# First K block ahead of the constants, issue time of transfers in the scheduler's costs, and the second K/V load behind a LayerNorm's rsqrt

## The chip, the cores and the metric

One core of a Trainium2 chip. The metric is the device time of one execution in microseconds. A run gives that time, the span between its first and last instruction (about 1.8 us less) and the mean clock that TensorE was granted, as a share of full speed.

## The reference, cut to what matters

The kernel computes the forward pass and all gradients of a gated block. The part that the change touches:

```python
xn = layernorm(A_q)                       # 2048 tokens x 512
k_shift = sum_t k_pad[:, t:t+S] * shift_k[:, 3-t]       # four taps along the tokens
kv = k_shift * v
y = irfft(rfft(kv, 2S) * rfft(ssm_k, 2S))[:S] + kv * ssm_D   # a long convolution for each channel
s = xn * y
h = sigmoid(xn @ w_gate) * (xn @ w_up)
out = A_q + s * silu(h @ w_down)
# and the gradients of q, k, v, shift_k, ssm_k, ssm_D, w_gate, w_up, w_down for a given grad_out
```

The Fourier transforms are matmuls against constants made on the chip. The 512 channels go in four groups of 128; the tokens in 16 blocks of 128.

## The kernel before

The kernel first records all its operations, then a list scheduler puts them into one order, with costs that its author wrote down; then it emits them. So any change of a cost or of the recorded order can deal the operations of all engines anew. The cost of a transfer, and when the scheduler believes it to have landed:

```python
def dcost(self, alt):
    ...                                   # nb bytes; run = contiguous bytes
    return (0.56 if eng == "gpsimd" else 0.4), d      # time on the issuing queue, time of the transfer

# in order():
    if op.dma:
        occ, d = self.dcost(alt)
        t = max(t, pipe - 9.0)
        pipe = max(pipe, t + 1.0) + d
        fin = pipe + 1.0
```

The start (K/V loads are issued by GpSimd; `after` is a value that a load waits for; the LayerNorm's rsqrt is a power on GpSimd):

```python
def ld_kv(cg, after=None):
    kh, vg = stA["kh", cg], stA["vg", cg] = kh_r.next(), vg_r.next()
    ...
    if after is not None:
        nc.vector.tensor_copy(kh[0:1, 3, 0:1], after)
        nc.vector.tensor_copy(vg[0:1, 0, 0:1], after)
    nc.gpsimd.dma_start(kh[:, 3:, :], kC[:, :, c0:c1])
    ...
    nc.gpsimd.dma_start(vg, vC[:, :, c0:c1])

def f_ln(i, part=None):
    ...
    nc.gpsimd.tensor_tensor(out=rstd_all[:, i:i + 1], in0=st[:, 8:9], in1=neghalf, op=ALU.pow)

ld_kv(0, wg[0:1, 2, 0:1])
ld_kv(1, wg[0:1, 2, 0:1])
...
make_identity(nc, ident)
f_ln(SEQ[0])
gen_fft_consts(nc, ar, ia, ib, negpi, Cf, BD, R)
f_ln(SEQ[1])
```

The convolution runs as streams side by side. Two of them: `acc` is one buffer: group 2's first multiply overwrites what group 1's store is still reading.

```python
def strK():
    for cg in range(NG):
        KT = stA.pop(("KT", cg))
        nc.vector.tensor_tensor(KT[:, 0:1], KT[:, 0:1], Dcol_b[:, cg:cg + 1], ALU.add)   # the D tap
        KC = KC_r.next()
        for jh in range(2):
            pt = ps_tr([8, 128], name="ps_kt")
            for jj in range(8):
                nc.tensor.transpose(pt[:, jj, :], KT[:, 8 * jh + jj:S:16], ident)
            nc.evac(KC[:, 8 * jh:8 * jh + 8, :], pt[:], 1024)
            yield 1024
        ...

def strV():
    for cg in range(NG):
        acc = acc_r.next()                                # the ring has one buffer
        for lag in (3, 2, 1, 0):
            ...
            if lag == 3:
                nc.vector.tensor_tensor(acc, src, skl, ALU.mult)
            else:
                nc.vector.tensor_tensor(term, src, skl, ALU.mult)
                nc.vector.tensor_tensor(acc, acc, term, ALU.add)
        nc.gpsimd.dma_start(ksh_d[cg], acc.rearrange("p j d -> p (j d)"))
        nc.vector.tensor_tensor(kvt, acc, vg, ALU.mult)
        ...                                               # step1, flip
```

## Time and profile before

| | before |
|---|---|
| time, 3 runs | 548.42 us (548.23 to 548.76) |
| span of the profiled run, clock | 546.9 us, 0.999 |
| TensorE idle, all | 26.6 us |
| of it 0 to 20 us | 7.7 us |
| of it 40 to 100 us | 7.4 us |
| longest pause of TensorE from 25 us to its last matmul | 0.9 us |

The lines behind these numbers stand in the prediction. From 200 to 520 us TensorE is busy 99%, and from 190 to about 385 us its order is the same in all kernels of the table below (each of its weight loads comes earlier or later by one and the same time, within 0.25 us).

Besides busy time I use one derived number below, the **lead**: the matmul work that TensorE has begun by a time T, in us, less what the kernel before has begun by then. It is counted from the weight loads, of which each trace without added matmuls has 5517, at 58 ns for a matmul of 128 columns and 216 ns for one of 512. A lead of 1.6 at 30 us means that TensorE is 1.6 us further in its work than the kernel before was at 30 us. Matmul records are not used for it: the trace before lacks 59 of them. The gaps that they leave count as idle time in the table above.

### The profile page before, as it was taken

How to read it: one execution, taken by the hardware profiler on the slowest of the kernel's cores; microseconds unless marked ns; L12 is line 12 of the kernel's file. 1: busy time of each engine (PE TensorE's matmuls, PEld its weight loads, DVE VectorE, ACT ScalarE, POOL GpSimd, SP SyncE). 2: the span in 40 equal slices, each digit the busy share in tenths (PEclk: the TensorE clock that was granted, in tenths of full speed). 3: DMA queues.
4: the chain of work that ended last, by engine and by line, in shares of the span. 5: the costliest groups of instructions: out<-in, count | busy, mean ns of one | idle time of the engine just before them, and what ended most of it. 6: DMA issues, size and time to landing. Idle time of an engine off the chain costs nothing.

```text
span 546.9 us, 13392 instructions
## 1 busy us (share of the span) xinstructions
PE 520.3 (95%) x5458; PEld 371.5 (68%) x5517; DVE 457.2 (84%) x841; ACT 347.1 (63%) x455; POOL 151.0 (28%) x260
## 2 busy tenths in 40 slices
PE   5899888999999999999999999999999999999996
PEld 3897787898688566777665666655766666665643
DVE  9699999767797998898989989829969999999550
ACT  8879899877886334544433345348777877765521
POOL 3626333304212222312222211220141051241221
PEclk9999999999999999999999999999999999999999
DMA  8999898867522998989979999999876479867422
GB/s 286 249 222 301 235 232 198 272 195 197 196 83 77 264 202 236 260 145 244 258 179 176 274 190 306 292 321 271 255 251 191 144 224 347 276 205 235 128 93 90
DMA packets 119007, 120.35 MB, mean 220 GB/s; under 512 B 76613, under 2 KB 97185, under 8 KB 118946
## 3 DMA queue, kind: packets, MB, share of 16 engines
q1 hardware_dynamic: 102514, 67.03, 50.4%
q0 software_dynamic: 15904, 52.47, 32.2%
q8 instruction: 43, 0.70, 0.5%
q14 instruction: 18, 0.15, 0.1%
q10 hardware_dynamic: 528, 0.00, 0.0%
HBM read 54.23 MB, written 47.55 MB: 186 GB/s over the span
## 4 chain that ended last, share of the span: by engine, by line
PE 66%; DVE 16%; issue 8%; ACT 5%; POOL 2%; DMA 1%; POOLq 0%; DVEq 0%; ACTq 0%
PE psum L519 66%; DVE slab L519 16%; ACT slab L519 5%; DMA ksh_d<-slab 1%; POOL out_dram L519 1%; POOL slab L519 1%; ACT L519 0%; POOLq L1451 0%; POOL KK_d L519 0%; POOLq L519 0%; DVEq L519 0%; ACTq L519 0%; POOLq L1440 0%
## 5 line engine op out<-in xcount | busy, mean ns | idle before, releaser
L519 PE MATMUL psum<-slab 128*128 128x128 bf16 (+3 forms) x5458 | 520.3, 256 | 21.7 <-ACT slab L519 11.5
L519 PEld LDWEIGHTS <-slab 128*128 128x128 bf16 (+2 forms) x5517 | 371.5, 102 | 170.1 <-issue 17.5
L519 DVE TENSOR_TENSOR slab<-slab 128x512 bf16<-128x512 bf16 (+7 forms) x467 | 300.1, 685 | 15.1 <-ACT slab L519 8.3
L519 ACT CAST slab<-psum 128x1024 bf16<-128x1024 f32 (+4 forms) x260 | 214.2, 866 | 80.2 <-PE psum L519 72.4
L519 ACT COPY slab<-psum 128x1024 bf16<-128x1024 bf16 (+2 forms) x82 | 68.5, 861 | 85.5 <-PE psum L519 85.2
L519 POOL DMA_DIRECT2D out_dram<-slab x75 | 44.9, 598 | 196.8 <-ACT slab L519 100.9
L519 DVE TENSOR_TENSOR slab<-psum,slab 128x512 bf16<-128x512 f32 (+3 forms) x84 | 63.7, 761 | 17.5 <-PE psum L519 10.0
L519 ACT ACTIVATE slab<-slab 128x512 bf16<-128x512 bf16 (+3 forms) x46 | 36.8, 805 | 18.4 <-DVE slab L519 17.8
L519 ACT ACTIVATE slab<-psum 128x512 bf16<-128x512 f32 (+1 forms) x64 | 37.3, 585 | 10.0 <-PE psum L519 8.1
L519 DVE SCALAR_TENSOR_TENSOR slab<-slab 128x1 f32<-128x1 f32 (+3 forms) x64 | 28.0, 438 | 15.7 <-ACT slab L519 12.5
L519 POOL DMA_DIRECT2D KK_d<-slab x32 | 17.3, 542 | 46.0 <-ACT slab L519 37.6
L519 DVE COPY slab<-psum 128x1024 bf16<-128x1024 bf16 (+2 forms) x34 | 21.0, 636 | 8.1 <-PE psum L519 7.8
L519 POOL DMA_DIRECT2D slab<-in_A_q_dram x29 | 16.0, 553 | 31.8 <-DMA out_dram<-slab 20.8
L519 DVE TENSOR_SCALAR slab<-slab 128x1 f32<-128x1 f32 (+7 forms) x72 | 20.5, 319 | 0.5 <-PE psum L519 0.2
L519 DVE CAST slab<-psum 128x1024 bf16<-128x1024 f32 (+1 forms) x13 | 14.8, 1141 | 4.7 <-PE psum L519 4.5
L519 DVE SCALAR_TENSOR_TENSOR slab<-psum,slab 128x512 f32<-128x512 f32 x16 | 11.0, 688 | 7.1 <-PE psum L519 6.9
L519 POOL DMA_DIRECT2D slab<-in_A_k_dram x16 | 14.9, 930 | 7.1 <-DVE slab L519 3.9
L519 POOL TENSOR_TENSOR slab<-slab 128x1 f32<-128x1 f32 x16 | 10.6, 663 | 13.6 <-DVE slab L519 13.3
L519 POOL DMA_DIRECT2D slab<-in_grad_out_dram x16 | 8.6, 539 | 17.7 <-DMA out_dram<-slab 11.6
L519 DVE BATCH_NORM_STATS2 slab<-slab 128x6 f32<-128x512 bf16 x16 | 10.9, 683 | 0.0
L519 POOL DMA_DIRECT2D slab<-sF_d x7 | 3.8, 537 | 22.7 <-DVE slab L519 18.5
L519 POOL MEMSET slab<- 1x384 bf16 (+3 forms) x16 | 5.9, 376 | 14.5 <-DVE slab L519 11.3
(21 smaller groups left out, 45.4 us busy)
## 6 DMA issues: line engine op xcount, KB each, us to landing
KK_d<-slab POOLq DMA_DIRECT2D x32, 256.0 KB, 4.0
slab<-KK_d SPq DMA_DIRECT2D x16, 512.0 KB, 6.5
out_dram<-slab POOLq DMA_DIRECT2D x58, 128.0 KB, 4.4
hS_d<-slab SPq DMA_DIRECT2D x16, 352.0 KB, 3.3
dgS_d<-slab SPq DMA_DIRECT2D x16, 352.0 KB, 3.9
duS_d<-slab SPq DMA_DIRECT2D x16, 352.0 KB, 3.7
slab<-in_A_k_dram POOLq DMA_DIRECT2D x8, 512.0 KB, 7.2
slab<-hS_d SPq DMA_DIRECT2D x8, 512.0 KB, 5.8
```

The source lines that it names most:

```text
L519: getattr(getattr(self.nc, eng), meth)(*[place(v) for v in a], **{x: place(v) for x, v in k.items()})
```

## The change

Its intent: give TensorE the first K block's transposes while the constants are still being made; tell the scheduler that a GpSimd issue with many short runs takes 1.17 us, not 0.56; and keep the second K/V load's two issues from standing in front of the first LayerNorm work that needs GpSimd.

```diff
+        soft = 0.56 if nb < 600 * run else 1.17
...
-        return (0.56 if eng == "gpsimd" else 0.4), d
+        return (soft if eng == "gpsimd" else 0.4), d
...
     ld_kv(0, wg[0:1, 2, 0:1])
-    ld_kv(1, wg[0:1, 2, 0:1])
...
     f_ln(SEQ[0])
+    nc.vector.tensor_tensor(stA["KT", 0][:, 0:1], stA["KT", 0][:, 0:1], Dcol_b[:, 0:1], ALU.add)
+    KC = stA["KC"] = KC_r.next()
+    for jh in range(2):
+        pt = ps_tr([8, 128], name="ps_kt")
+        for jj in range(8):
+            nc.tensor.transpose(pt[:, jj, :], stA["KT", 0][:, 8 * jh + jj:S:16], ident)
+        nc.evac(KC[:, 8 * jh:8 * jh + 8, :], pt[:], 1024)
...
     f_ln(SEQ[1])
+    ld_kv(1, rstd_all[0:1, SEQ[1]:SEQ[1] + 1])
...                                  # in strK: the add and the transposes only for cg > 0
```

Below, A is the K block's work ahead, B the issue time, C the second load behind the rsqrt.

More of the change, by code (lines that the diff above doesn't have):

```diff
@@ L917, in strK @@
             KT = stA.pop(("KT", cg))
-            nc.vector.tensor_tensor(KT[:, 0:1], KT[:, 0:1], Dcol_b[:, cg:cg + 1], ALU.add)
-            KC = KC_r.next()
-            for jh in range(2):
+            if cg > 0:
+                nc.vector.tensor_tensor(KT[:, 0:1], KT[:, 0:1], Dcol_b[:, cg:cg + 1], ALU.add)
+            KC = KC_r.next() if cg > 0 else stA["KC"]
+            for jh in range(2 if cg > 0 else 0):
                 pt = ps_tr([8, 128], name="ps_kt")
```

## The prediction

> **What bounds the kernel now.** I read the busy shares first.
>
> ```profile
> PE 520.3 (95%) x5458; PEld 371.5 (68%) x5517; DVE 457.2 (84%) x841; ACT 347.1 (63%) x455; POOL 151.0 (28%) x260
> ```
>
> TensorE (PE) is busy for 520.3 of 546.9 us, so 26.6 us is all its idle time: no change of order can win more unless it also makes matmuls run closer together. The next question is where the 26.6 us lie. The table of busy time by stretches gives it (columns after the stretch: its length, then busy us and instructions of PE, PEld, DVE, ACT, POOL, then granted clock, DMA share, GB/s):
>
> ```profile
> 0.00:10.00 10.00, 3.64 (x20) 2.11 (x20) 9.01 (x34) 7.65 (x8) 3.73 (x16) 1.00 0.73 255
> 10.00:20.00 10.00, 8.62 (x121) 7.93 (x119) 7.34 (x34) 8.35 (x10) 7.06 (x6) 1.00 1.04 294
> ...
> 50.00:60.00 10.00, 8.30 (x103) 6.66 (x103) 10.00 (x12) 9.22 (x11) 3.29 (x7) 1.00 0.88 298
> ```
>
> The first 20 us lack 7.7 us of PE (10 - 3.64 and 10 - 8.62). In 40 to 100 us PE lacks another 7.4 us with VectorE (DVE) at 92 to 100%: there PE waits for the two engines that empty PSUM. From 200 to 520 us PE is at 98.7 to 100% and lacks 3.3 us; the last 27 us lack 5.0. So the change, whose named parts all lie in the first 25 us, works on the largest gap.
>
> Next, the instructions of that stretch in order of time, engine by engine (start, busy us, engine, operation, count, idle before it and what ended the idle):
>
> ```profile
> 8.97 3.43 ACT L519 ACTIVATE slab<-slab 128x2048 bf16<-128x2048 int32 x3 [0.81 <-DVE slab L519]
> 12.47 1.01 ACT L519 COPY slab<-psum 128x1024 bf16<-128x1024 bf16 x1
> ...
> 19.31 0.81 ACT L519 ACTIVATE slab<-slab 128x512 bf16<-128x512 bf16 x1 [1.22 <-DVE slab L519]
> 20.14 1.28 ACT L519 ACT_TABLE_LOAD   x1
> ```
>
> ```profile
> 12.75 1.20 POOL L519 DMA_DIRECT2D slab<-in_A_k_dram  x1
> 13.94 2.28 POOL L519 DMA_DIRECT2D slab<-in_A_v_dram  x1
> 16.20 1.15 POOL L519 DMA_DIRECT2D slab<-in_A_k_dram  x1
> 17.34 1.15 POOL L519 DMA_DIRECT2D slab<-in_A_v_dram  x1
> 18.51 0.57 POOL L519 TENSOR_TENSOR slab<-slab 128x1 f32<-128x1 f32 x1
> ```
>
> ```profile
> 16.31 3.45 PE L519 MATMUL psum<-slab 128*128 128x128 bf16 x59 [0.31 <-DMA slab<-in_A_ssm_k_dram]
> 20.18 1.63 PE L519 MATMUL psum<-slab 128*128 128x128 bf16 x25 [0.42 <-ACT slab L519]
> 22.56 2.62 PE L519 MATMUL psum<-slab 128*128 128x128 bf16 x42 [0.76 <-ACT slab L519]
> ```
>
> The reader is to see one chain. The 0.57 us instruction at 18.51 is the power -1/2 (the rsqrt) of the second token block's LayerNorm. Its input was ready when DVE had added epsilon, about 15.5, but GpSimd (POOL) works in order and was issuing four K/V loads. DVE then waited 2.38 us for the rsqrt (to 19.12), ScalarE (ACT) 1.22 us for DVE; the normalised block was done at 20.12, the PE transposed it at 20.18, ACT loaded the sigmoid table, and the next PE work began at 22.56. The chain that ended last agrees: it runs through DVE to 16.15, POOL 16.20 to 19.09, DVE, ACT to 22.52, PE.
>
> **What the Trainium skill says.** "PSUM — Partial Sum Buffer", section "Engine vs sequencer instructions", has the ACT, DVE and GpSimd queues strictly first in, first out; the trace agrees, as the rsqrt stood 3 us behind two load issues it does not need. "SBUF — State Buffer", section "Who interferes with whom", has GpSimd blocked while DVE uses a two-port mode for copies and tensor_scalar; the issue at 13.94 took 2.28 us against 1.15 to 1.20 for its three likes, while DVE ran small copies and tensor_scalars, which fits. "ScalarE: Activation LUTs", section "What ACT_TABLE_LOAD costs", gives 1283 ns for a load; the trace has 1.28 us, at 20.14, and this stays.
>
> **The change part by part.**
>
> *Second load behind the rsqrt.* In the built program after, POOL has the rsqrt of block two directly after the first V load, and the second K and V issues behind it. That takes 1.15 + 1.15 = 2.3 us from in front of it: it can start when the issue of 13.94 ends, about 16.2, and end at 16.8. Its statistics also move up on DVE (ahead of the mask multiply), so the input is no bound. The second K/V data come later by about the rsqrt, 0.6 us: issues at 17 and 18.2, landing after about 10 us (10.0 and 10.4 before), so by 29; the second V group starts its arithmetic on DVE only after the first group's, whose own first multiply is at 30.59. Hidden, with over 10 us to spare.
>
> *K transposes and D-tap ahead.* The 0.15 us add moves on DVE from 10.30 to about 7.8; K block 0, issued at 1.56 and landing 4.5 to 6.5 us later, has arrived by 8.1 at the latest. Sixteen transposes follow, so PE gets K work in the gap that ended at 8.22, and ACT copies the first half between the two large sine activations, filling the 0.81 us in which it waited for DVE. But this is a move, not a removal: before the second LayerNorm ACT has, before and after, two sines of 2.0, one of 0.8, one normalisation of 0.8, five copies of 1.0 and one of 0.6. Summing from 6.16 with no gaps: 2.0 + 1.0 + 0.8 + 1.0 + 2.0 + 0.8 + 0.6 + 3.0 = 11.2, so 17.4, and with 0.6 for the first copy's wait for transposes, about 18.0. DVE also takes two first-step evictions (1.22 us each by the row of float casts) in place of cheaper copies; its queue from 11.4 on (where its float constants were done before) is then 1.2 for an eviction, 1.1 for the statistics and small copies, 1.2 for the other eviction, 0.8 for the mask multiply and 0.7 + 0.8 for the thirteen small constants, which ends near 17.2, behind the rsqrt. So ACT, not the rsqrt, becomes the last of the chain: the second normalisation starts near 18.1 instead of 19.31.
>
> Sum at the start: 19.31 - 18.1 = 1.2 us. In addition PE has about eight more 58 ns matmuls (59 in 3.45 us) behind it at the point where it transposes block two (143 against 135 in the built order), another 0.5. That is 1.2 to 1.7 us earlier into a stage that is then PE- or DVE-bound, and all of it should reach the end, because nothing after it is tied to an absolute time.
>
> *Issue time in the order.* This changes no instruction, only what the list scheduler believes an issue costs on POOL when there are 600 or more runs: 1.17 us for 0.56. The trace says the new figures are true:
>
> ```profile
> L519 POOL DMA_DIRECT2D KK_d<-slab x14 | 7.6, 543 | 10.7 <-ACT slab L519 10.6
> L519 POOL DMA_DIRECT2D slab<-in_A_k_dram x2 | 2.4, 1182 | 4.0 <-DVE slab L519 3.9
> ```
>
> It bears on the strided K, V, and paired output transfers. In the built programs PE's order of operations is identical from about 45 to 85% of its instructions; the first 45% (the convolution with the forward half) and the last 15% are dealt anew. In the first of these PE idles some 10 us in all outside the start (1.2 from 20 to 40, 7.4 from 40 to 100, 2.0 from 100 to 200); a better-timed order could win 1 to 2, a worse one lose as much. I put +0.5 us of gain on it, for truer figures and for K work running ahead, which feeds the flips and the spectral products earlier. In the tail the last 60 or so matmuls are the same and back to back, so nothing large.
>
> Together: 1.5 + 0.5 = 2.0 on 548.42, so 546.4; I lean a little further, to 546.0, because the K load of block two can also be issued some 2 us earlier (it was issued at 12.47, when block 0's transposes were done) and a wait of PE at 16.31 ended with that load.
>
> **The rivals.** First, the wait is replaced one for one: ACT or the DVE constants simply end the same chain at 19, and the gain is under 0.5 us: 548. For it speaks that ACT and DVE are both 80% busy or more in the first 20 us; against it, ACT had 1.22 + 0.81 + 0.35 us of idle time there, which are removed. Second, the first 1.5 us are won but the redealt first 45% loses them, because DVE is full from 50 us on, so that an early K stream only fills PSUM and waits: 548 to 550. For it speaks DVE at 100% in 50 to 60 us; against it, DVE is only 68% busy in 20 to 30, so its queue too can begin earlier. Third, the redealt order happens to fit much better, and half of the 7.4 us of 40 to 100 us goes: 542 to 543. For it speaks that POOL's order was made with a wrong cost; against it, POOL is only 28% busy and waits mostly for ACT and DVE. Fourth, K block 0 lands late and the early add stalls DVE and all constants behind it; the landing times above make this at most some tenths.
>
> **Range and chances.** The start is worth 0.5 to 2.5 us, the redealt order +2 to -3, which gives 542 to 549 for 8 in 10. Two per cent is 11 us: it would take over 40% of PE's idle time to be faster by that, and a new stall of a kind that I see no cause for to be slower. Faster 0.03, same 0.95, slower 0.02.
>
> **What would show it.** Right: the second normalisation on ACT starts at 17.5 to 18.7; POOL's rsqrt stands before the second K issue and no longer makes DVE wait 2 us; the PE stretch without gaps that began at 22.56 begins near 21; PE busy stays at 518 to 521 and the idle sum falls by about 2; from 200 us on all is the same but shifted. Wrong: DVE idle near 7.8 behind K block 0; the idle of 40 to 100 us above 8 or below 5; a new wait of V group two for its data near 40 us.

## The result, and the profile after

The changed kernel took 547.54 us (546.69 to 548.90, four runs) against 548.46 us (548.23 to 548.76) in the same rounds: a ratio of 0.9985, 95% interval 0.9964 to 1.0006. Ratios here are taken from the runs of the same rounds, so not quite the ratio of the medians that I quote. The interval holds 1, so these four runs alone show no difference. The gain of the medians is 0.9 us where 2.4 were forecast; the time lies in the forecast range. Two repeats (below, `again` and `again2`) put it at 1.7 and 0.1 us.

The start first. The busy time by stretches of the changed kernel (length, busy us and instructions of PE, PEld, DVE, ACT, POOL, then granted clock, DMA share, GB/s):

```profile
0.00:10.00 10.00, 4.04 (x25) 2.67 (x26) 9.02 (x35) 7.68 (x9) 4.17 (x16) 1.00 0.74 255
10.00:20.00 10.00, 8.09 (x125) 7.80 (x123) 9.07 (x35) 9.21 (x10) 5.46 (x6) 1.00 1.02 295
50.00:60.00 10.00, 7.10 (x92) 5.76 (x90) 9.97 (x12) 9.72 (x13) 4.95 (x8) 1.00 0.95 265
```

And the changed kernel's instructions in order of time, ScalarE, GpSimd and TensorE (start, busy us, engine, operation, count, idle before it and its cause):

```profile
17.36 1.02 ACT L520 COPY slab<-psum 128x1024 bf16<-128x1024 bf16 x1
18.26 0.83 ACT L520 ACTIVATE slab<-slab 128x512 bf16<-128x512 bf16 x1
```

```profile
16.20 0.74 POOL L520 TENSOR_TENSOR slab<-slab 128x1 f32<-128x1 f32 x1
18.36 1.19 POOL L520 DMA_DIRECT2D slab<-in_A_k_dram  x1 [1.41 <-DVE slab L520]
```

```profile
13.62 1.07 PE L520 MATMUL psum<-slab 128*128 128x128 bf16 x16 [0.80 <-DVE slab L520]
15.80 14.41 PE L520 MATMUL psum<-slab 128*128 128x128 bf16 x249 [1.11 <-DVE slab L520]
```

The second LayerNorm's normalisation, at 19.31 before, is at 18.26 (forecast: near 18.1); ScalarE reaches it without idle, so ScalarE's own work is now the last of the chain, as forecast. The rsqrt is at 16.20, two us before the second load's issue. From 15.80 TensorE runs without a pause past 30 us (the view ends there), where before it stopped at 20 and 22 us. The lead is 1.62 us at 30 us: in the forecast "1.2 to 1.7". So the start came out as forecast; whether for the forecast reason, the parts alone will show.

Then 50 to 60 us: TensorE is busy 7.10 us where it was 8.30. The pauses, of TensorE in the changed kernel:

```profile
55.03 0.59 PE L520 MATMUL psum<-slab 128*128 128x512 bf16 x2 [1.00 <-ACT slab L520]
57.53 2.73 PE L520 MATMUL psum<-slab 128*128 128x512 bf16 x29 [1.91 <-DVE slab L520]
...
102.51 1.68 PE L520 MATMUL psum<-slab 128*128 128x128 bf16 x23 [1.55 <-DVE slab L520]
```

The kernel before has no pause this long after 25 us. The lead over the run: 1.62 at 30 us, 2.32 at 50, 0.30 at 65, 3.82 at 100, 1.80 at 110, 1.14 at 190 and 1.58 at 500. Between 190 and 460 us each operation of TensorE comes earlier than before by the same time, 1.34 us within 0.04. So what is left at 190 does reach the end unchanged, and the start's 1.6 us is almost gone at 65. That the lead at the end is again about the start's is no proof that it is the same 1.6 us: the redealt order between gains and loses more than that.

The pause at 102.51 is another transfer: VectorE waits 1.74 us, to 101.17, for a block of x issued at 95.78. In `again` the same place cost some 0.3 us of lead, not 2.0, so it varies from run to run.

### The profile page after: what moved, and what is told of

Its sections match the earlier page's. It is cut to its first block, busy times and chain, and to the rows that moved or that the text cites. A ratio compares the mean times of both kernels' runs of the same rounds, so it can differ in the third digit from the quotient of the medians.

```text
span 545.7 us, 13451 instructions
## 1 busy us (share of the span) xinstructions
PE 522.2 (96%) x5517; PEld 371.1 (68%) x5517; DVE 459.1 (84%) x839; ACT 349.1 (64%) x457; POOL 150.5 (28%) x260
## 4 chain that ended last, share of the span: by engine, by line
PE 73%; DVE 11%; issue 8%; ACT 3%; DMA 2%; POOL 2%; POOLq 0%; DVEq 0%; ACTq 0%
PE psum L520 73%; DVE slab L520 11%; ACT slab L520 3%; POOL out_dram L520 1%; DMA ksh_d<-slab 1%; DMA slab<-in_A_q_dram 1%; POOL slab L520 0%; POOL KK_d L520 0%; POOLq L1460 0%; POOL sF_d L520 0%; POOL hF_d L520 0%; POOLq L520 0%; DVEq L520 0%; ACTq L520 0%; POOLq L1449 0%
## 5 line engine op out<-in xcount | busy, mean ns | idle before, releaser
L520 PE MATMUL psum<-slab 128*128 128x128 bf16 (+4 forms) x5517 | 522.2, 257 | 18.2 <-DVE slab L520 10.5
L520 DVE TENSOR_TENSOR slab<-slab 128x512 bf16<-128x512 bf16 (+6 forms) x467 | 300.4, 686 | 10.2 <-ACT slab L520 4.8
L520 ACT CAST slab<-psum 128x1024 bf16<-128x1024 f32 (+5 forms) x255 | 210.0, 861 | 79.4 <-PE psum L520 70.8
L520 ACT COPY slab<-psum 128x1024 bf16<-128x1024 bf16 (+2 forms) x88 | 74.9, 868 | 87.5 <-PE psum L520 87.3
L520 ACT ACTIVATE slab<-slab 128x512 bf16<-128x512 bf16 (+3 forms) x47 | 37.8, 807 | 15.3 <-DVE slab L520 14.7
L520 POOL DMA_DIRECT2D KK_d<-slab x32 | 19.3, 632 | 48.4 <-ACT slab L520 33.0
L520 DVE CAST slab<-psum 128x1024 bf16<-128x1024 f32 (+1 forms) x18 | 20.9, 1163 | 4.9 <-PE psum L520 4.0
L520 DVE COPY slab<-psum 128x1024 bf16<-128x1024 bf16 (+2 forms) x28 | 16.9, 623 | 6.5 <-PE psum L520 6.4
L520 POOL TENSOR_TENSOR slab<-slab 128x1 f32<-128x1 f32 x16 | 13.3, 844 | 15.4 <-DVE slab L520 15.2
L520 POOL DMA_DIRECT2D slab<-in_A_v_dram x6 | 7.9, 1323 | 2.5 <-DVE slab L520 1.3
```

The costliest lines, as they stand in the source:

```text
L520: getattr(getattr(self.nc, eng), meth)(*[place(v) for v in a], **{x: place(v) for x, v in k.items()})
```

## The experiments

Eighteen experiments ran, all with a correct result. Two questions were asked. What does each part do alone? And where does the lead go after 30 us?

| kernel | parts | time, us: median (range) | ratio to before, 95% | lead at 30 / 65 / 100 / 500 us |
|---|---|---|---|---|
| again | ABC | 546.90 (546.30 to 548.66) | 0.9973 [0.9953, 0.9992] | 1.45 / -0.57 / 3.26 / 2.66 |
| again2 | ABC | 548.26 (546.88 to 550.01) | 0.9983 [0.9948, 1.0018] | 1.45 / -0.86 / 2.58 / 2.01 |
| p_A | A | 551.13 (550.84 to 552.19) | 1.0043 [1.0023, 1.0064] | 0.41 / -0.71 / -1.22 / -3.02 |
| p_B | B | 547.09 (546.16 to 551.12) | 0.9982 [0.9955, 1.0009] | 1.91 / 0.15 / 3.82 / 2.44 |
| p_C | C | 549.32 (546.92 to 552.84) | 1.0011 [0.9979, 1.0042] | 1.68 / -2.55 / -1.10 / -1.30 |
| p_AB | AB | 549.14 (546.64 to 553.14) | 1.0011 [0.9978, 1.0045] | 1.59 / -0.46 / 2.46 / 0.71 |
| p_AC | AC | 548.35 (547.89 to 548.97) | 0.9991 [0.9976, 1.0006] | 0.12 / 0.19 / 1.19 / 0.05 |
| p_BC | BC | 554.22 (547.49 to 556.36) | 1.0064 [1.0024, 1.0104] | 1.33 / -4.00 / -6.14 / -7.72 |
| n1 | none; 0.58 for 0.56 | 546.55 (546.40 to 551.29) | 0.9971 [0.9943, 0.9999] | 0.00 / 0.00 / 2.78 / 2.22 |
| n5 | none; 0.26 for 0.25 | 548.62 (548.07 to 550.26) | 1.0000 [0.9981, 1.0018] | 0.06 / -0.49 / 0.66 / 0.22 |

The lead is that of the one profiled run, which need not be a median run; the profiled run of p_BC counts as slow (its time, 556.36, is over 1.5% above the fastest of that kernel), its five fast runs, 547.5 to 554.7, are what its ratio rests on.

### The change again

`again` and `again2` are the changed kernel, nothing edited.

> The changed kernel again, unaltered, for a narrower interval. From the two traces: PE is 1.6 us of matmul work ahead of the kernel before at 25 to 35 us, 3.8 ahead at 100 us, 1.8 ahead at 105 us, 1.3 to 1.5 ahead from 150 us to the end. Theory (the start is won and a stall near 101 us gives most of the rest back): 546.6 to 547.6 us, 0.9 to 1.9 us under the kernel before. Rival (the gain is run-to-run noise of the granted clock, 0.995 in three of the four runs): the interval contains no difference.

> The changed kernel unchanged, beside the three with fills. Both theories: runs with a mean clock of .999 or more at a span near 545.0, the others (.994 to .996) at 545 to 547; median 546.8 to 547.5.

Measured: 546.90 and 548.26 us. `again2`'s clocks are mixed: one run at 1.0 (span 545.1), the others at .991 to .997 (545.3 to 548.2); its median lies above the forecast 546.8 to 547.5. Of the three intervals only that of `again` lies wholly below 1. So the gain is small and unsteady.

### Each part alone, and two at a time

```diff
# p_A:  only the lines of the change in the start and in strK
# p_B:  only
+        soft = 0.56 if nb < 600 * run else 1.17
-        return (0.56 if eng == "gpsimd" else 0.4), d
+        return (soft if eng == "gpsimd" else 0.4), d
# p_C:  only
-    ld_kv(1, wg[0:1, 2, 0:1])
+    ld_kv(1, rstd_all[0:1, SEQ[1]:SEQ[1] + 1])     # moved behind f_ln(SEQ[1])
```

> Only the K transposes and the D-tap ahead. In the built order ScalarE here runs two sigmoids ahead of the second LayerNorm, which VectorE makes instead, although the rsqrt still stands behind four load issues. Theory (what wins the start is the table load and the first sigmoids ahead of the late rsqrt): PE 1.2 to 2.0 us ahead at 30 us. Rival (the rsqrt's place on GpSimd is what counts): no lead at 30 us, within 0.4. At the end: 546.5 to 548.5 in either, by how the rest is dealt.

> Only the new issue time in the order. Theory: the second LayerNorm's rsqrt still waits behind four load issues on GpSimd, so PE's lead at 30 us is 0 within 0.4 us, and any difference at the end (within 1.5 us either way) is made after 30 us by the redealt order. Rival (the truer cost lets the scheduler deal a better convolution stage): PE 1 us or more ahead at 190 us, 547.4 or less.

> Only the second K/V load behind the rsqrt. In the built order the second LayerNorm stands ahead of the table load on ScalarE, as in the kernel before, but the rsqrt comes two load issues (2.3 us) earlier. Theory (the start is held by the table load and sigmoids behind ScalarE's queue of copies, not by the rsqrt): lead of PE at 30 us 0 to 0.8. Rival (my prediction: the rsqrt was the chain's wait): lead 1.0 to 1.7 us. End: 547 to 549.

> The two source moves (K transposes with D-tap ahead; second K/V load behind the rsqrt) without the new issue time in the order. Theory (the start's gain comes from these two, the issue time only redeals the order): PE 1.2 to 1.9 us ahead at 30 us, as in the changed kernel; the time anywhere from 545.5 to 548 by how the order is dealt. Rival (the issue time is what makes the gain): no lead at 30 us, 548 or more.

> Two of three parts: K block 0's work ahead and the issue time, second K/V load where it was. Theory (the true issue time is what moves the start, in whatever company): lead of TensorE over the kernel before of 1.2 to 2.0 us at 30 us, median 547.0 to 547.8. Rival (a redealt order is worth anything from -2.5 to +1.5 us whatever was the reason to deal it anew): no particular number, 546.5 to 551; the early K work alone cost 2.5 us and could do so again (549.5 to 551).

> Issue time and the second K/V load behind the rsqrt, K block 0's work where it was. Theory: both take the same wait (VectorE's for the rsqrt) off the path, so they don't add: lead at 30 us 1.7 to 2.2, not 3.6; median 546.7 to 547.3, as the issue time alone (547.09). Rival (they add): lead 3 us or more, 545.5. Rival (redealing): 547 to 550, and a wait of VectorE at the landing of the first group's spectra store says why.

Measured: the table. Three things follow.

First, each of B and C wins the start alone (1.91 and 1.68 us at 30 us), and together they don't add (1.33, and 1.62 with A). C does it as forecast. B does it otherwise: the rsqrt is still late in p_B, but with issues that it knows to be long, the scheduler gives the second block's normalisation to VectorE, so that ScalarE, with the table load and two sigmoids, waits for no rsqrt. ScalarE and then VectorE in p_B:

```profile
17.79 1.28 ACT L520 ACT_TABLE_LOAD   x1
19.08 1.08 ACT L520 ACTIVATE slab<-psum 128x512 bf16<-128x512 f32 x2
```

```profile
19.30 0.41 DVE L520 TENSOR_SCALAR slab<-slab 128x512 bf16<-128x512 bf16 x1
```

Second, A wins little at the start (0.41, and 0.12 with C), and alone the kernel is slower by 2.5 us; why is open. K work in an early gap of TensorE is not what the start's gain came from. Nor do the two source moves A and C together make it, as was forecast: p_AC has both, and its rival came true (no lead, 548 us or more). Its second normalisation starts at 17.21, a microsecond earlier than in the changed kernel. But it still waits 1.54 us for VectorE, and an accumulator copy (the CAST at 17.93) that TensorE needs stands behind it. ScalarE and TensorE in p_AC:

```profile
17.21 0.81 ACT L519 ACTIVATE slab<-slab 128x512 bf16<-128x512 bf16 x1 [1.54 <-DVE slab L519]
```

```profile
18.97 11.26 PE L519 MATMUL psum<-slab 128*128 128x128 bf16 x190 [1.03 <-ACT slab L519]
```

So the start of the normalisation does not set the lead; what ScalarE has to hold back for it does. In the changed kernel two accumulator copies of ScalarE (at 16.45 and 17.36) stand ahead of it.

Third, the end does not follow the start. p_C changes nothing in the order of TensorE and ScalarE, and little on VectorE and GpSimd; its lead of 1.68 us is -2.55 at 65 us. p_BC loses 5.3 us between 30 and 65, behind a pause of 3.31 us that ends on ScalarE; what dealt it so is open. All of the six but p_B came out slower than their theories forecast.

### Is it the true figure, or any figure?

B's gain could come from 1.17 us being true, or from the cards being dealt anew. Two controls deal them anew with figures that have no truth in them:

```diff
# n1
-        return (0.56 if eng == "gpsimd" else 0.4), d
+        return (0.58 if eng == "gpsimd" else 0.4), d
# n5
-LATE = 0.25
+LATE = 0.26
```

> Control: the kernel before with the scheduler's cost of every GpSimd issue 0.58 us for 0.56, a change with no truth in it, that deals most of TensorE's order anew all the same. Theory (the issue time of the change gains because 1.17 is true, and puts the sigmoids ahead of the late LayerNorm): no start gain, lead at 30 us within 0.5 of 0, median 548.0 to 549.3. Rival (redealing alone moves the time by as much as the change did): median off the kernel before by 0.9 us or more, either way.

> Second control: the kernel before with the scheduler's share for late transfers 0.26 for 0.25; a different order again, no truth in it. Theory: lead at 30 us within 0.5 of 0, median 548.0 to 549.3. Rival: off the kernel before by 0.9 us or more, either way.

Measured: n1 546.55 us, as good as anything, with no start gain at all (lead 0.00 at 30 and at 65 us); n5 548.62, as before. My theory falls here: the truth of the figure is not needed for the gain. n1 wins its time between 65 and 100 us. The stretches of the kernel before, then of n1:

```profile
85.00:90.00 5.00, 4.03 (x49) 2.99 (x48) 4.97 (x7) 4.76 (x8) 2.12 (x4) 1.00 0.64 215
90.00:95.00 5.00, 4.07 (x51) 3.38 (x51) 5.00 (x9) 5.00 (x8) 2.17 (x5) 1.00 1.16 195
```

```profile
85.00:90.00 5.00, 4.68 (x62) 3.78 (x61) 4.76 (x8) 5.00 (x8) 2.73 (x5) 1.00 0.83 271
90.00:95.00 5.00, 5.00 (x73) 4.39 (x72) 4.85 (x8) 4.95 (x7) 1.49 (x3) 1.00 1.24 137
```

TensorE's busy time in these 10 us goes from 8.10 to 9.68. The order alone, at one meaningless step of 0.02 us, moves the time by -2.2 us; over all the kernels of the table it goes from -2.2 to +5.5 (n1 and p_BC, medians against 548.74 of the kernel before in the same rounds). The change's own effect is inside that.

### Where the lead goes: a store that VectorE waits for

In the changed order VectorE begins channel group 2 at 47.4 us; before it was at 52.1. Its first multiply overwrites `acc`, so it has to wait until group 1's store of 512 KB has landed. VectorE at that place in the three profiled runs of the changed kernel (after, again, again2):

```profile
47.41 2.48 DVE L520 TENSOR_TENSOR slab<-slab 128x2048 bf16<-128x2048 bf16 x2 [0.24 <-DMA ksh_d<-slab]
```

```profile
48.22 2.48 DVE L520 TENSOR_TENSOR slab<-slab 128x2048 bf16<-128x2048 bf16 x2 [0.91 <-DMA ksh_d<-slab]
```

```profile
48.71 2.48 DVE L520 TENSOR_TENSOR slab<-slab 128x2048 bf16<-128x2048 bf16 x2 [1.40 <-DMA ksh_d<-slab]
```

The store was issued at 41.12, 41.28 and 41.27 and landed at 47.38, 48.20 and 48.69. TensorE's pause 10 us later is 1.91, 2.59 and 3.09 us: each time 1.7 us more than VectorE's wait. So the store adds 0.2 to 1.4 us to a pause of 1.7 us that the changed order has in any case. What TensorE waits for is an accumulator that VectorE empties (at 56.26 in the profiled run), and that stands behind the last three of group 2's operations:

```profile
53.26 3.09 DVE L520 TENSOR_TENSOR slab<-slab 128x2048 bf16<-128x2048 bf16 x3
56.26 1.22 DVE L520 TENSOR_TENSOR slab<-psum,slab 128x1024 bf16<-128x1024 f32 x1
```

VectorE has no break from 47.41 on (9.97 of the 10 us from 50 to 60). The landing of a transfer is a time of the kind that the prediction had ruled out; the full VectorE is what its second rival had named.

One experiment came upon it by accident. It was meant to take away the wait at 101 us, by putting the statistics that wait for the x block behind another VectorE operation:

```diff
# bn_late, in emit(): the order of the change, with one operation moved
+        at = {s[0].n: i for i, s in enumerate(seq)}
+        seq.insert(at[1653], seq.pop(at[2807]))
```

> The changed kernel with one VectorE instruction moved by two places: the LayerNorm statistics at 101.17 us, which waited 1.74 us for its block's load while it held up everything behind it, now stand behind the next two eviction multiplies. Nothing else is moved. Theory (this head-of-line wait took the lead of 3.8 us down to 1.8): PE's wait of 1.55 us near 102 us shrinks to under 0.5 and PE stays 2.8 us or more ahead at 110 us; the time falls 1.0 to 1.5 us under the changed kernel, to about 546. Rival (the convolution stage is paced by VectorE and ScalarE in any order, and the wait only shows slack that is lost elsewhere): the lead at 150 us is again 1.3 to 1.5 and the time is that of the changed kernel within 0.4.

Measured: 548.94 us (546.65 to 550.68), ratio 1.0000 [0.9978, 1.0022]. In its profiled run the same store, issued at 40.84, landed at 51.40. VectorE, TensorE, and the stretch after it:

```profile
51.42 2.48 DVE L523 TENSOR_TENSOR slab<-slab 128x2048 bf16<-128x2048 bf16 x2 [4.55 <-DMA ksh_d<-slab]
```

```profile
54.56 1.04 PE L523 MATMUL psum<-slab 128*128 128x128 bf16 x15 [3.18 <-DVE slab L523]
```

```profile
55.00:60.00 5.00, 3.74 (x30) 2.68 (x30) 4.96 (x7) 4.24 (x6) 1.62 (x3) 0.66 0.84 292
```

The moved operation comes 50 us later, so this is the variation of the landing, not the edit. The pause at 102 us is gone (none over 0.9 us there), but the time is no better than the changed kernel's. The last line is new: the granted clock of TensorE, the third number from the end, is 0.66.

The wait can be taken away with another buffer. There is no room for a second `acc`, but the part of `y2A` that group 4 will write is free until then:

```diff
# acc2 (on the change) and B_acc2 (on p_B): orders kept, groups 2 and 4 accumulate elsewhere
+            alt = y2A[:, :, 3 * GW:4 * GW]
...                                   # for odd cg, acc -> alt in the multiplies, the adds, the store and kvt
```

> The changed kernel in exactly its own order of instructions, but the shifted-K accumulator of the second and fourth channel group lies in a stretch of the output array that is not written until the end of this stage. So the second group's first multiply no longer has to wait for the store of the first group's accumulator to land. In three executions of the changed order that wait was 0.24, 0.91 and 4.55 us, with PE idle up to 3.2 us and the granted clock at 0.66 to 0.90 for 15 us after it in the longest. Theory (this landing is what makes the changed kernel lose its lead in part of its executions): VectorE waits 0 there, the granted clock is 0.998 or more, the spread between executions shrinks to about 0.6 us, spans 544.3 to 545.3, so 546.1 to 547.1 in time, 1.5 to 2.5 under the kernel before. Rival (the lost lead comes from elsewhere): spans still spread from 544.5 to 547.

> The kernel with only the new issue time, in its own order, with the same second place for the accumulator. Its second group started 2.0 us after the store had landed (50.34 against 48.37), so theory: no change in most executions, 546.5 to 547.2, and no execution over 548. Rival (the second place itself helps or costs): differs from the issue time alone by over 0.5 us in the best executions.

Measured: acc2 547.32 us (547.01 to 552.55), ratio 0.9987 [0.9955, 1.0020]; B_acc2 547.03 (546.91 to 547.15), 0.9966 [0.9945, 0.9987]. In acc2 VectorE starts group 2 at 47.23 without a wait, though the store landed at 48.63. Five of its six spans lie within 545.2 to 546.2, the sixth is 550.8. The median is not better, the forecast clock of 0.998 was not met (0.994 to 0.996), and the lead at 65 us is again negative, about -1.0. TensorE still pauses at 54 to 57 us, 1.04 us and then

```profile
57.35 4.85 PE L526 MATMUL psum<-slab 128*128 128x512 bf16 x38 [1.58 <-DVE slab L526]
```

and a spell at half clock follows (57 to 60 us; below). So without the wait for the store the 1.7 us of pause are still there, and the loss too: the wait adds to the pause and varies, but it is not the cause of the whole. B_acc2 did as forecast, all runs below 548; its best run is 0.75 us above p_B's best, which the rival had asked for, but the medians agree and the two ran on different chips.

### The clock

Sixteen runs of the changed kernel (after, again, again2) and 58 of the kernel before from the later rounds, by their mean clock:

| | clock .998 or more | below |
|---|---|---|
| before | 53 runs, mean span 546.9 us | 5 runs, 548.2 us |
| changed | 5 runs, mean span 545.0 us (544.5 to 545.7) | 11 runs, 546.5 us (544.9 to 548.2) |

In the profiles the cause of a low mean is plain: slices of 1 us show either 1.00 or, in spells of 3.4 or 6.8 us, 0.50. There is none in the middle of before, p_B, p_AB, p_AC, B_acc2, n1, n5 or the three of the changed kernel. There are spells at 55 and 62 us in bn_late, 57 in acc2, 83 in p_A, 56 to 62 in p_C, 61 and 78 to 84 in p_BC, each at or behind pauses of TensorE. In p_C, TensorE first and then the stretch; and the same stretch of before:

```profile
56.99 3.57 PE L519 MATMUL psum<-slab 128*128 128x128 bf16 x32 [2.52 <-DVE slab L519]
```

```profile
55.00:60.00 5.00, 3.01 (x29) 3.01 (x29) 5.00 (x6) 2.21 (x4) 1.33 (x3) 0.60 0.89 343
```

```profile
55.00:60.00 5.00, 3.87 (x59) 3.55 (x59) 5.00 (x6) 4.72 (x6) 0.91 (x2) 1.00 0.72 241
```

p_C does half of the matmuls in these 5 us, of which the pause takes 2.0. Its spell runs from 55.97 to 62.80. The 5.8 us of it that lie behind the pause cost 2.9 us of work (half clock while TensorE is idle anyway costs nothing), the greater part of the 4.2 us that its lead loses between 30 and 65 us. And p_C's pause too is VectorE's wait for the store: 2.28 us, to 52.84. Its TensorE order is that of the kernel before; it only came to this place earlier, and the store landed later (52.81 against 50.68).

The clock is not the only thing that scatters: the kernel before has runs 2 to 5 us slower than its median at a mean clock of 0.998 or more (550.90, 551.00 and 552.95 us), and p_B has one (551.12). What those are is open.

The Trainium skill has this on the page "TensorE: Matmul & The Clock Gate", section "What's actually happening": the array's clock is halved after an idle window of about 3.4 us and released after a busy one, and the window runs freely, not from the kernel's start. How far the traces agree stands at the end of this part. I had not looked there for the prediction, since the view of the kernel before shows nothing but 1.00. That column misses the start: the clock record begins at 13.13 us there, and up to that time matmuls of 128 columns start 0.107 us apart, afterwards 0.056.

Does the pause bring the half clock, or do they only go together? First try: fill the pauses with matmuls that nothing reads.

```diff
# after_fill, C_fill, BC_fill, in emit(): before the operation that waits, into a free accumulator bank (cut: where none is free, as transposes into its own bank)
+                    for _ in range(FILL[op.n]):
+                        self.nc.tensor.matmul(self.psum[:, b * 512:b * 512 + 128], self.ident, self.ident, start=True, stop=True)
```

> The changed kernel, every order kept, with 14 and 30 matmuls of 58 ns that nothing reads in TensorE's pauses of 1.0 and 1.9 us at 54 and 55.6 us. Theory (the pause brings the half clock): all six runs at .998 or more, spans 544.7 to 545.7, median 546.7 or below, and again2 has runs at .996 or less that this has not. Rival (the clock falls for another reason): the same mix of clocks, some of them at .994 to .996, and a median like again2's.

> p_C with 30 such matmuls in its pause of 2.2 us at 54.8 us. p_C had a spell of 6.6 us at half clock, 3.3 us of work lost, and runs at .992 to .995 in four of six. Theory: no spell at 55 to 63 us, five or six runs at .998 or more, spans 545.1 to 546.3, median 546.9 to 548.0; the lead at 65 us is 0 to 1.7 in place of -2.55. Rival: spell and spread as in p_C, median 549.3.

> p_BC with 46 and 64 such matmuls in its pauses of 3.3 and 4.2 us at 58.5 and 75 us. p_BC's profiled run had spells of 3.4 and 6.7 us at half clock behind them, 5 us of work lost; the pauses themselves stay. Theory: clock .997 or more, spans 547 to 550, median 549 to 551.5 in place of 554.2. Rival: clock and median as p_BC's.

Measured: after_fill 549.68 us (548.26 to 550.60), C_fill 551.73 (548.22 to 556.09), BC_fill 554.70 (551.39 to 557.83). None is faster than the kernel it was made of, so by times and mixed clocks the theory got no support. The profiles say why this was a poor test. In after_fill the pause stood one matmul ahead of the place filled: 2.54 us of idle TensorE, then 30 useless matmuls after it, and a spell of 3.4 us. A fill is work in the wrong place whenever the pause is not where it was in the profile from which I took it. Where the fill did meet the pause, in the profiled run of BC_fill, TensorE ran 64 of them from 74.83, and 75 to 85 us are at 1.00, where p_BC, idle for 4.2 us, has 6.8 us at half clock. That is one pair of runs, the p_BC one slow. The profiled run of C_fill agrees: 30 fills from 56.24, no spell, clock 0.999 and a lead of 0.5 us at 65 us (forecast 0 to 1.7; p_C had -2.55). But VectorE's wait for the store was shorter there too (0.66 us), and three of its six runs still have 0.993.

Second try: make pauses where nothing else changes, in the kernel before between 221 and 360 us, by letting TensorE wait for ScalarE's copies.

```diff
# pause: at five places of the order
+        self.nc.tensor.matmul(ps[0], self.ident, self.ident, start=True, stop=True)
+        for _ in range(copies):                       # 3, 6, 9, 13, 18
+            self.nc.scalar.copy(self.cell, ps[0])
+        self.nc.tensor.matmul(ps[1], self.ident, self.cell, start=True, stop=True)
```

> The kernel before, its order kept, with five pauses of TensorE near 221, 251, 281, 311 and 340 us: it waits for 3, 6, 9, 13 and 18 small copies of ScalarE (estimate, 0.3 us each: 1.3, 2.2, 3.1, 4.3 and 5.8 us). Theory (a pause of some 2 to 3 us or more is enough): spells at 0.50 behind the last three or four, 3.3 us or more each, that start within 4 us of the pause; none behind the first. The time is before's plus the pauses (up to 17 us) plus 1.7 us for each spell, 565 to 573. Rival (the clock falls for another reason): no spell, clock .998 as before's, and time before's plus the pauses alone.

Measured: 570.32 us (570.07 to 571.59) against 548.16. The five waits of TensorE, and the stretches behind the third and fourth:

```profile
222.64 0.22 PE L521 MATMUL psum<-slab 128*128 128x128 bf16 x1 [0.95 <-ACT slab L518]
...
254.61 0.22 PE L521 MATMUL psum<-slab 128*128 128x128 bf16 x1 [1.84 <-ACT slab L518]
...
287.77 0.22 PE L521 MATMUL psum<-slab 128*128 128x128 bf16 x1 [2.74 <-ACT slab L518]
...
323.26 0.27 PE L521 MATMUL psum<-slab 128*128 128x128 bf16 x1 [3.93 <-ACT slab L518]
...
359.98 0.27 PE L521 MATMUL psum<-slab 128*128 128x128 bf16 x1 [5.85 <-ACT slab L518]
```

```profile
288.00:293.00 5.00, 5.00 (x64) 5.00 (x62) 2.86 (x8) 1.51 (x4) 0.00 (x0) 0.66 0.00 0
323.00:327.00 4.00, 3.74 (x14) 1.74 (x14) 1.27 (x3) 0.80 (x2) 0.15 (x1) 0.57 0.96 299
```

The pauses sum to 15.3 us; the time rose by 22.2. Behind the third pause, and from within the fourth and fifth, the clock is at 0.50 for 3.4, 3.4 and 6.8 us; none follows the first two. What the spells cost shows in the weight loads, which fall behind those of the kernel before by 1.22, 2.12, 4.63, 5.76 and 7.93 us at the five places. Beyond its pause that is 0.27 and 0.28 us for the first two, which have no spell (the added matmuls and copies), and 1.89, 1.83 and 2.08 us for the others. So the three spells cost about 1.6, 1.6 and 1.8, or 5.0 of the 6.9 us that the pauses leave open; the last one has 2.8 of its 6.8 us inside the pause, where half clock costs nothing. (The 6.8 us that the next forecast names counts that part too.) This is the cause shown: a pause put in at a quiet place brings the spell, and the spell costs time beyond the pause.

Its twin should have had the same waits with TensorE busy in them:

```diff
# pause_fill
+        for _ in range(fills):                        # 14, 30, 46, 66, 98
+            self.nc.tensor.matmul(ps[2], self.ident, self.ident, start=True, stop=True)
```

> The twin of pause: the same five waits for ScalarE, with 14, 30, 46, 66 and 98 matmuls of 58 ns in them that nothing reads. Theory (it is the idleness that brings the half clock): no spell behind any of them, clock .998, and the time is before's plus the five waits alone, 548.2 + 15.3 = 563.5 (562.5 to 564.5), 6.8 below pause. Rival (the wait, or what it does to the other engines, lowers the clock, or costs the 6.8 us by itself): spells and time as in pause, 570.3.

Measured: 584.23 us (582.12 to 586.12). Neither theory: the fills did not run in the pauses but behind them, since `ps[2]` lies in the bank that ScalarE was reading and had to wait for it too. The kernel has the same five pauses, then 254 more matmuls (14.2 us at 0.056 us each), and spells of 3.4 and 6.8 us at the fourth and fifth pause only; what lies of them behind the pauses costs at most 3.8 us: 548.2 + 15.3 + 14.2 + 3.8 = 581.5, with 2.7 us not accounted for. It adds one fact. The third pause, of 2.73 us, has no spell here:

```profile
290.99 2.73 PE L520 MATMUL psum<-slab 128*128 128x128 bf16 x46 [2.73 <-ACT slab L518]
```

So a pause of 2.7 us may or may not bring one, which fits a window that runs freely. The kept traces show the window itself. In each of the eight profiles with more than one stretch at half clock (the one behind the last matmul counts) they start whole multiples of 3.413 us apart (in pause at 288.92, 323.05 and 357.18: ten each time), so they lie on a grid that the pauses do not shift. I cut each of the twenty traces into windows on that grid, from 22 us to 8 us before its end (where there is no spell, the half clock behind the last matmul gives the grid), and summed TensorE's idle time in each:

| run | window, us | TensorE idle in it, us | clock after it |
|---|---|---|---|
| acc2 | 53.86 to 57.27 | 2.54 | 0.50 |
| pause, third pause | 285.51 to 288.92 | 2.27 | 0.50 |
| p_A | 79.69 to 83.10 | 1.99 | 0.50 |
| again2 | 56.94 to 60.36 | 1.90 | 1.00 |
| pause_fill, third pause | 286.69 to 290.10 | 1.85 | 1.00 |
| pause, second pause | 251.38 to 254.79 | 1.84 | 1.00 |
| p_C | 52.56 to 55.97 | 1.81 | 0.50 |

Of the windows at full clock, all twelve with 1.99 us of idle time or more bring half clock in the next, and of those below none does but p_C's. So it is the idle time within one window that counts, in one piece or in two; a window's edge cuts 0.5 us off the third pause in pause, and 0.9 us in pause_fill. The profiled runs of the changed kernel reach 1.63, 1.85 and 1.90 us, close to that edge, so that some of its runs can have a spell and others none. A clean twin, with the same wait and TensorE busy in it, is still missing.

## Why the prediction was wrong

**What was right.** The bound, and the waits of the first 23 us in the kernel before. The second normalisation at 18.26 (18.1); ScalarE as the new last of the chain; the rsqrt ahead of the second load; K/V data hidden, though issued at 18.36 and 19.54 (17 and 18.2); no stall at the early add (it ran at 7.62); a lead of 1.62 us at 30 us, against 1.2 to 1.7. From 190 to 460 us all is the same but shifted. No 2% either way.

**What was right by luck.** The 1.2 to 1.7 us were to come from the two source moves through an earlier normalisation. C alone gives 1.68, but both together without the issue time (p_AC) give 0.12 us with the normalisation at 17.21; the issue time alone, for which nothing was forecast at the start, gives 1.91 us with the rsqrt as late as before. So the size was met, but not by the two moves as they were summed. The stretch of TensorE without gaps, forecast to begin near 21, began at 15.80.

**The step that failed** is "all of it should reach the end, because nothing after it is tied to an absolute time". The start's 1.62 us is 0.30 at 65 us, -0.57 and -0.86 in the repeats. The redealt order begins group 2's arithmetic 4.7 us earlier. On a full VectorE it then stands ahead of an accumulator that TensorE waits for: 1.7 us of pause, 1.58 in acc2 with no wait for the store. And it begins onto the landing of a store that the old order left 1.4 us of room (landed 50.68, first multiply 52.07): 0.2 to 1.4 us more, by when the store lands. In p_C, which keeps the old order of TensorE, the store and the half clock behind the pause do it almost alone (2.28 us of wait). Pauses of 1.9 to 3.1 us bring TensorE near the edge at which the clock is halved. By 100 us the profiled runs of the changed kernel, none of which has a spell, have won the lead back (2.6 to 3.8 us), and 1.6 to 2.7 us is left at 500. So what the median lacks is less the 2 us at 65 than the half clock that such pauses bring in other runs.

**The sum, term by term.** Forecast: 1.5 for the start, 0.5 for the redealt order, 0.4 as a lean, 2.4 together. Measured: in the five runs with a clock of .998 or more the changed kernel gains 546.9 - 545.0 = 1.9 us of span, close to the 2.0 without the lean; in the other eleven 0.4 (546.9 - 546.5). Eleven of sixteen runs at 1.5 us less make 1.0 us lost on average, and the gain over all sixteen is 1.0 us (547.0 - 546.0). So the term left out has the size of the gain itself. Where the eleven runs lost it is not seen in them, as they have no profile; that it is pauses and half clock (one spell of 3.4 us costs up to 1.7 us) is concluded from the profiled kernels and from pause, not shown.

**"This changes no instruction"**, said of the issue time, was right, but as a term of 0.5 us it was the least understood. Alone it makes the start's whole gain by another way than the source moves, and n1 shows a gain of 2.2 us from a figure that means nothing. The second rival, a redealt 45% that gives the start's gain back because VectorE is full from 50 us on, came closest. It had the place and the larger part of the pause; it had neither the store nor the half clock. The third rival, that a better order takes half of the 7.4 us of 40 to 100 us, happened in n1 (4.9 us left), not in the change (6.1, 7.1 and 7.5 us left in its three profiled runs).

**Best version.** None beats the changed kernel's clean runs clearly. n1 (five runs of six at 546.4 to 546.8, one at 551.3) and B_acc2 (all six within 546.91 to 547.15) have intervals below the kernel before, n1's barely (0.9999); of the two, B_acc2 is the steady one.

## What to carry to other kernels

When a scheduler deals the order anew, a gain at the start is only a loan: look for buffers that the new order reuses sooner, and ask of each whether the transfer that still reads it has landed; and look at what now stands ahead of the work that the busiest engine waits for. Before crediting a change of a cost figure with a gain, run the same kernel with a meaningless change of the same figure; here that moved the time by as much. And count pauses of TensorE that come near 2 us within 3.4 us as longer than they are: here up to 1.7 us, half of a spell of 3.4 us, came on top, in some runs and not in others.

## What the Trainium skill lacked or had wrong

- "TensorE: Matmul & The Clock Gate", "What's actually happening": it has the half clock after an idle window of about 3.4 us, free-running. The traces agree on the length and the free run (spells start whole multiples of 3.413 us apart). But the window need not be wholly idle: 1.99 us of idle TensorE in it was enough (p_A), 1.90 was not (again2), and in p_C 1.81 was. The spells lasted 3.4 or 6.8 us at 0.50.
- "DMA: Bandwidth & Descriptors", "Anatomy of one DMA — SWDGE (gpsimd) path": by its fit of 2.0 us plus bytes at 436 GB/s (estimate from that page: 3.2 us) a store of 512 KB is quick. Among other traffic the store here took 6.3 us (41.12 to 47.38), 7.4 (again2), 10.6 (bn_late, 40.84 to 51.40) and 11.5 (p_C, 41.34 to 52.81) from issue to landing. A buffer's reuse is better planned on the worst of these.
- The same section calls descriptor generation small and variable. GpSimd was held 0.54 us by an issue of a 128-row transfer and 1.15 to 1.20 us by one of 2048 short runs; the section has no figure for how it grows with the number of runs.
- No page that I found says how much the landing of one and the same transfer varies between executions; here it decided between a pause of 1.9 and one of 3.1 us.
